# GpSimd starts with a sum over partitions before it makes the unit matrix; transposes are planned longer; the plan is searched anew

## The chip, the cores and the metric

The kernel runs on one core of a Trainium2 chip. The metric is the device time of one execution in microseconds (us); several executions are timed, and the median is the figure. One further execution is recorded by the hardware profiler, and the views shown here come from it. The engines are TensorE (PE in the profile; its weight loads are PEld), VectorE (DVE), ScalarE (ACT), GpSimd (POOL) and SyncE (SP), whose queue issues all of this kernel's DMAs.

## The reference

Causal attention in blocks of 64 over 8 batches, 8 heads, 576 positions and head width 64, then a feed-forward of two matrix products with the gate h * tanh(softplus(h)) between them, in float32:

```python
def _attn_ref(q, k, v):                       # (8, 8, 576, 64) each
    scores = scale * np.matmul(q, k.transpose(0, 1, 3, 2))
    mask = block_i >= block_j                 # blocks of 64 positions
    scores = np.where(mask, scores, -1000000000.0)
    scores = scores - np.max(scores, axis=-1, keepdims=True)
    attn = np.exp(scores)
    attn = attn / (np.sum(attn, axis=-1, keepdims=True) + 1e-09)
    return np.matmul(attn, v)

def _moe_ref(x, w_in, w_out):                 # (4608, 512), (512, 2048), (2048, 512)
    h = x @ w_in
    sp = np.where(h > 20.0, h, np.log1p(np.exp(np.minimum(h, 20.0))))
    return (h * np.tanh(sp)) @ w_out
```

The two weight matrices arrive as 64-bit words; the kernel makes float32 values of them with integer operations.

## The kernel before

**Work.** Most matrix products are done in float16 with each operand split into a high and a low half (hi and lo): three products hi*hi, hi*lo, lo*hi stand for one. Each batch has four pairs of heads and two tiles of tokens (384 and 192 columns). The first batch is computed in float32 from the loaded data directly (`attend`: scores by query L993, far blocks L1005, scores by key L1064 and L1075, subtraction of the maxima L1103, exponentials on ACT L1121, values L1136). The seven later batches go through `attend_pair`: scores S on PE (L1199, L1211), row maxima on DVE (L1240 to L1248), exponentials on ACT (L1274), the high half (L1306 or L1311; DVE, POOL or ACT) and the low half on DVE (L1323), a transpose by DMA into `PT` (L1330) and a shorter one into `PL` (L1345), and the products U with the values (L1378). Then `weigh` divides by the sums on DVE (L1441, L1442) and writes `xt`, which a DMA transposes into `x` (L1511). The feed-forward of a tile is 192 matmuls per product: `m1` (L1556), the gate on ACT (L1585), the split `Gt` on ACT or DVE (L1617, L1626, L1632), `m2` (L1661), scaling (L1693 or L1700) and a store (L1718).

**Beginning.** `make_identity` on POOL makes the unit matrix: a fill with zeros (masks.py:197) and a select that sets the diagonal (masks.py:199). ACT makes two scaled copies of it (L532), one of which, `unit_msc`, is an operand of the subtraction L1103, so PE needs it for the first pair of heads. `batch(0)` sums the squares of the first batch's v: four squares on ACT (L735), then `partition_all_reduce` on POOL adds over the partitions (L744), then DVE makes a power of two of the sum (L748, L500, L510, L750; the operation `sx`). `weight` unpacks the weights: a DMA (L574), integer operations on DVE (L583, L600), squares on ACT (L611), another sum over partitions on POOL (L619), and the halves.

**Order.** A planner sets the order of every engine before the program is built. Each operation is given an engine, a duration and the operations it waits for:

```python
unit = add("pool", 9.4, lambda: make_identity(nc, ident))
...
red = add(
    "pool", pool(4), lambda: nc.gpsimd.partition_all_reduce(TT, T, P, RED.add), sq
)
```

`pool(4)` is 0.36. `Plan.order` walks through a model of the engines and takes, on each engine, the operation with the earliest due time among those that are ready; the due times come from the table `DUE`, one number for each part of the work, and several passes backward and forward refine them. What comes out is one list in order of time, emitted operation by operation: each engine executes its own in that order and does not pass over one that waits. The DMAs' durations in the plan are pairs: the issue time on SP and the transfer's share. `TURN` is for L1330, `TURN_LATE` for L1345, `TURN_X` for L1511.

Of the kernel before, what the change touches and what calls it, by code (L numbers as in the profile page):

```python
# [18 lines left out]
RED = bass_isa.ReduceOp  # L19

P = 128
# [6 lines left out]


DUE = {  # L30
    "w": ((-46.5, 68, 288.5, 132.5), (84, 351, 228, 284.5)),
    "batch": (176, 189, 314.5, 356.5, 530.5, 736, 535.5, 733),
    "load": (
        (60.5, -52, 273, 25),
        (-74.5, 81, 78.5, -54),
        (131, 403, 308, 368.5),
        (569, 364, 410, 435),
        (393, 574, 501.5, 383.5),
        (328, 572.5, 376, 468.5),
        (511.5, 532.5, 550, 604.5),  # L40
        (521.5, 578, 675.5, 773),
        (693, 782, 838.5, 623.5),
    ),
    "tile": (
        (-92.5, -99.5, 300, -90, -20.5, -14, -31.5, -26.5,
         22, 41.5, 203.5, 303, 83.5, -150.5, 74,
         156, 263.5, 52, 27, 285, 347, 454.5),
        (332.5, 10.5, 149, 111.5, 49.5, -23.5, 20, 112,
         148, 283, 374, 296.5, 96.5, 280.5, 93,
         272.5, 290.5, 333, 290, -21.5, 267, 58),  # L50
        (122, 28.5, 413.5, 462, 420, 703.5, 334, 357.5,
         353.5, 489.5, 547, 334.5, 397.5, 225, 303,
         171, 141.5, 393, 382, 458.5, 344.5, 288),
        (665, 61, 275.5, 79.5, 406, 276, 121, 559.5,
         142, 287.5, 302.5, 256, 547.5, 15, 239.5,
         339.5, 587, 305.5, 448.5, -37, 343.5, -260.5),
        (431.5, 448, 421, 352.5, 342.5, 304.5, 403, 280.5,
         452.5, 381, 353, 234.5, 266, -52.5, 212,
         451, 597, 430.5, 440, 297, 529, 487.5),
        (90.5, 357.5, 294.5, 366, 432, 586, 536, 506,  # L60
         584, 735, 559.5, 416.5, 634, 158, 409.5,
         653, 530, 646.5, 728, 300.5, 486, 68),
        (309.5, 378, 316, 336, 489.5, 256.5, 472, 388.5,
         270, 382.5, 410.5, 511, 497.5, -59, 303,
         478, 329, 516, 402, 550.5, 630.5, 632),
        (302, 325.5, 413.5, 281.5, 390, 474, 385.5, 471.5,
         328.5, 503, 638, 491, 500, -43, 689.5,
         465, 559, 580.5, 654, 269.5, 538, 7.5),
        (493, 348.5, 293, 300, 436, 484, 596, 563.5,
         416.5, 612, 746.5, 722, 812.5, 325.5, 803,  # L70
         488, 963.5, 797.5, 736.5, 549.5, 775, 672.5),
        (514.5, 599.5, 599.5, 700, 394, 645.5, 485, 778.5,
         694.5, 844, 648.5, 631, 557, -15.5, 763,
         558.5, 600.5, 798, 580.5, -68.5, 863, -79.5),
        (858, 832, 1077.5, 882, 682, 597.5, 632, 518.5,
         727, 922, 619, 604, 917, 319, 736.5,
         958, 741.5, 957.5, 600, 661.5, 648, 614),
        (645, 469.5, 526, 1034.5, 571, 716.5, 659, 647,
         604.5, 695.5, 689, 937, 843.5, -29.5, 773.5,
         940, 1047, 695.5, 648.5, 33, 896, 35.5),  # L80
        (738.5, 602.5, 621, 678, 542, 802, 585.5, 742,
         641.5, 717.5, 619, 772.5, 950, -62.5, 740,
         894, 1029.5, 870, 758, 1016, 770.5, 1018),
        (526, 570.5, 622.5, 567.5, 569.5, 735, 846, 816,
         827, 703, 845, 749, 914, -106.5, 942,
         868, 751, 786, 699.5, -119, 1010, 10.5),
        (966.5, 995, 813, 775.5, 1067.5, 797, 1013, 1076,
         1058.5, 1155, 1276.5, 1076, 745, 30, 1197.5,
         930, 789.5, 731, 775.5, 812, 904.5, 1154),
        (796, 962.5, 907.5, 817.5, 832.5, 995, 1051, 918,  # L90
         1190.5, 1054.5, 973.5, 1032.5, 1147.5, 2, 1185,
         968.5, 1204, 994, 1112.5, 61, 1279.5, -130),
    ),
}

# [27 lines left out]
class Plan:  # L123
# [31 lines left out]
    def add(self, eng, us, emit, after=(), take=(), free=(), other=(), table=None, psum=False):  # L155

        self.ops.append(Op(eng, us, emit, after, take, free, self.due, other))
        self.ops[-1].psum = psum
        self.ops[-1].table = table
        self.ops[-1].slack = self.slack * (eng == "pe")  # L160
        return self.ops[-1]
# [186 lines left out]
def attention_moe(  # L348
# [17 lines left out]
    nc = tc.nc  # L366
# [104 lines left out]
    wmax = dv[0][:, 12:13]  # L471
# [23 lines left out]
    add = plan.add  # L495
# [31 lines left out]
    ident, *diag = (f[:, i * P : (i + 1) * P] for i in range(3))  # L527
    minus = P2[1][:, 6 * P : 7 * P]
    plan.part("w", 0, 0)
    unit = add("pool", 9.4, lambda: make_identity(nc, ident))  # L530
    units = [
        add("act", 0.2, lambda o=o, s=s: nc.scalar.mul(o, ident, s), [unit])  # L532
        for o, s in ((minus, -1.0), (unit_msc, -MSC))
# [1193 lines left out]


    SLACK = 0.7
    TURN, TURN_LATE, TURN_X = (2.15, 0.8), (1.3, 0.3), ((3.2, 1.2), (1.5, 0.5))  # L1730
    heads, tiles = {}, []

    own = [load_own(p) for p in range(NP)]
# [97 lines left out]
```

## Time and profile before

| what | value |
|---|---|
| median of 3 runs | 1016.55 us (1016.04 to 1018.67) |
| the profiled execution's own time | 1016.76 us |
| its span | 1014.9 us |
| granted TensorE clock, mean of the span | 0.991 |
| busy: PE, DVE, ACT, POOL | 985.0, 668.6, 651.1, 81.6 us |

The profiled execution lasts 1.9 us longer than its span (what lies around the first and last instruction of the program), and 0.2 us longer than the median of the runs. "Busy" leaves out the instructions that only wait, branch or issue; the releaser behind an idle time in square brackets is the instruction whose end let the engine go on, and "issue" means that the profile shows nothing that was waited for. In rows of a window come the window, its length, then busy time and number of instructions of PE, PEld, DVE, ACT and POOL, the mean granted clock of TensorE, the busy share of the 16 DMA engines and GB/s.

### The profile page before, as it was taken

The page shows a single profiled execution, that of the slowest core. Times are in us where ns is not written, and L with a number is a line of the kernel's source. Part 1 is how long each engine was busy: PE and PEld are TensorE (multiplying, and loading weights), DVE is VectorE, ACT ScalarE, POOL GpSimd, SP SyncE. Part 2 cuts the span into 40 slices and gives each one's busy share as a digit, 9 for nine tenths or more (in the row PEclk, how much of TensorE's full clock was granted, in tenths as well). Part 3 has the DMA queues.
Part 4 walks back from the last instruction along what each step waited for, and adds up shares of the span by engine and source line. Part 5 has one row for each costly group of instructions (what it writes and reads, how often), then busy time and mean ns, then how long its engine had stood idle before and what let it go on. Part 6 is the DMA issues. An engine that isn't in the chain of part 4 may idle for free.

```text
span 1014.9 us, 25319 instructions
## 1 busy us (share of the span) xinstructions
PE 985.0 (97%) x10856; PEld 732.5 (72%) x10856; DVE 668.6 (66%) x1299; ACT 651.1 (64%) x1028; POOL 81.6 (8%) x110
## 2 busy tenths in 40 slices
PE   5899899999999999999999999999999999999998
PEld 3668567686678676777777966887677776786687
DVE  2999998897687747971788877683779646120200
ACT  2578887758877856882868696585657755323221
POOL 0000221210000000110011100000011000000000
PEclk9899999999999999999999999999999999999999
DMA  8683656897487426790587746472577551240000
GB/s 275 206 252 94 176 105 135 180 167 156 86 159 159 90 52 151 161 176 24 100 170 150 172 98 134 106 140 61 113 165 149 101 105 41 37 87 1 16 17 25
DMA packets 276849, 121.58 MB, mean 120 GB/s; under 512 B 224513, under 2 KB 262913, under 8 KB 276737
## 3 DMA queue, kind: packets, MB, share of 16 engines
q1 hardware_dynamic: 276736, 119.96, 54.2%
q8 instruction: 85, 1.39, 0.6%
q14 instruction: 28, 0.22, 0.1%
HBM read 55.18 MB, written 9.44 MB: 64 GB/s over the span
## 4 chain that ended last, share of the span: by engine, by line
PE 81%; DVE 10%; issue 3%; ACT 2%; DMA 2%; SPq 1%; POOL 0%; ACTq 0%; DVEq 0%; POOLq 0%
PE acc L1661 32%; PE acc L1556 32%; PE u L1378 7%; PE ss L1199 5%; DVE P L1323 1%; DVE pv L1240 1%; DVE Gt L600 1%; PE ss L1064 1%; PE u L1136 1%; DVE Gt L1632 1%; DMA VL<-in_v_dram 1%; PE acc L664 1%; DVE wo_l L691 1%; DMA PL<-P 1%; DMA PT<-P 1%
## 5 line engine op out<-in xcount | busy, mean ns | idle before, releaser
L1556 PE MATMUL acc<-x,wi_h 128*128 128x192 f16 (+1 forms) x2048 | 395.5, 287 | 1.3 <-DMA x<-xt 1.3
L1661 PE MATMUL acc<-Gt,wo_h 128*128 128x192 f16 (+1 forms) x2048 | 385.6, 286 | 0.5 <-DVE Gt L1632 0.5
L1556 PE MATMUL acc<-x,wi_l 128*128 128x192 f16 (+1 forms) x1024 | 293.8, 287 | 0.0
L1661 PE MATMUL acc<-Gt,wo_l 128*128 128x192 f16 (+1 forms) x1024 | 292.9, 286 | 0.0
L1556 PEld LDWEIGHTS <-wi_h 128*128 128x128 f16 x2048 | 191.0, 98 | 82.2 <-issue 7.0
L1661 PEld LDWEIGHTS <-wo_h 128*128 128x128 f16 x2048 | 187.6, 98 | 52.8 <-issue 2.7
L1585 ACT ACTIVATE Et<-acc,bv 128x384 f32<-128x384 f32 x192 | 109.4, 579 | 136.2 <-PE acc L1556 135.1
L1632 DVE SCALAR_TENSOR_TENSOR Gt<-Et,bv,Gt 128x1536 f16<-128x1536 f32 (+1 forms) x64 | 92.4, 1448 | 129.4 <-ACT Gt L1617 128.8
L1274 ACT ACTIVATE pe<-ss,pv 128x192 f32<-128x192 f32 (+1 forms) x280 | 147.8, 606 | 16.9 <-DVE P L1323 8.9
L1661 PEld LDWEIGHTS <-wo_l 128*128 128x128 f16 x1024 | 100.2, 98 | 34.1 <-issue 1.2
L1556 PEld LDWEIGHTS <-wi_l 128*128 128x128 f16 x1024 | 100.4, 98 | 33.7 <-issue 0.9
L1240 DVE TENSOR_REDUCE pv<-ss 128x2 f32<-128x384 f32 (+4 forms) x140 | 105.9, 789 | 20.2 <-PE ss L1211 19.1
L1323 DVE TENSOR_TENSOR P<-pe,P 128x1024 f16<-128x1024 f32 x84 | 102.3, 1220 | 13.7 <-ACT P L1311 9.4
L1378 PEld LDWEIGHTS <-PT 128*128 128x128 f16 x2352 | 79.7, 98 | 7.8 <-issue 2.4
L1378 PE MATMUL u<-VH,PT 128*128 128x65 f16 x1568 | 82.8, 194 | 2.5 <-DVE tt L1442 2.4
L1274 ACT ACT_TABLE_LOAD x56 | 71.8, 1283 | 13.3 <-DVE pv L1248 8.7
L1378 PE MATMUL u<-VO,PT 128*128 128x64 f16 x784 | 79.4, 193 | 0.0
L1585 ACT ACT_TABLE_LOAD x58 | 74.4, 1283 | 1.0
L1617 ACT ACTIVATE Gt<-Et,bv 128x768 f16<-128x768 f32 (+1 forms) x46 | 57.1, 1241 | 12.1 <-PE acc L1661 11.1
L1700 ACT ACTIVATE ot<-acc,bv 128x384 f32<-128x384 f32 (+1 forms) x35 | 16.9, 505 | 63.9 <-PE acc L1661 56.7
L1306 POOL CAST P<-pe 128x1024 f16<-128x1024 f32 x29 | 34.6, 1193 | 198.7 <-ACT pe L1274 102.8
L1199 PEld LDWEIGHTS <-QH 64*128 64x128 f16 x896 | 27.5, 94 | 27.5 <-issue 15.5
(127 smaller groups left out, 994.5 us busy)
## 6 DMA issues: line engine op xcount, KB each, us to landing
out_dram<-ot SPq DMA_DIRECT2D x48, 192.0 KB, 2.1
wo_l<-in_w_in_dram SPq DMA_DIRECT2D x8, 1024.0 KB, 5.2
Gt<-in_w_out_dram SPq DMA_DIRECT2D x16, 512.0 KB, 4.2
kl<-in_v_dram SPq DMA_DIRECT2D x28, 288.0 KB, 3.1
ql<-in_q_dram SPq DMA_DIRECT2D x28, 288.0 KB, 3.0
kl<-in_k_dram SPq DMA_DIRECT2D x28, 288.0 KB, 3.4
VL<-in_v_dram SPq DMA_DIRECT2D x28, 192.0 KB, 2.6
VL<-in_v_dram SPq DMA_DIRECT2D x28, 96.0 KB, 2.9
```

What stands on the lines that cost most here:

```text
L1199: nc.tensor.matmul(ss[:, 512 * a + col : 512 * a + col + n], lhsT=m[q_][hs, at : at + P], rhs=m[k_][hs, key : key + n], start=first, stop= ...
L1240: nc.vector.reduce_max(out=mx[:, c], in_=ss[:, :, c0:c1], axis=mybir.AxisListType.X)
L1274: nc.scalar.activation(pe[ex[r].slot][:, cols], ss_[S0[r].slot % NSS][:, cols], AF.Exp, scale=esc, bias=mx[:, c, a : a + 1],)
L1306: return lambda: op(out=both()[0], in_=both()[2])
L1323: lambda both=both: nc.vector.tensor_sub(both()[1], both()[2], both()[0]),
L1378: nc.tensor.matmul(out, lhsT=p_, rhs=v_, start=first, stop=True, skip_group_check=True,)
L1556: nc.tensor.matmul(pt, lhsT=w[:, d, f * P : (f + 1) * P], rhs=x[:, d, :], start=k == 0 and d == 0 and z == 0, stop=d == NP - 1 and z == 2, ...
L1585: nc.scalar.activation(Et[:, (self.i * NG + g) % NE, j : j + K, 0:n], acc_[c.slot % NACC][:, 0 : K * n].rearrange("p (k n) -> p k n", k=K) ...
L1617: lambda g_hi=g_hi, ev=ev: nc.scalar.activation(g_hi, ev, AF.Copy, scale=self.s_g),
L1632: lambda g_hi=g_hi, g_lo=g_lo, ev=ev: nc.vector.scalar_tensor_tensor(out=g_lo, in0=ev, scalar=self.s_g, in1=g_hi, op0=ALU.mult, op1=ALU.su ...
L1661: nc.tensor.matmul(pt, lhsT=w[:, f, o * P : (o + 1) * P], rhs=g, start=k == 0 and f == 0 and z == 0, stop=f == NF - 1 and z == 2, skip_gro ...
L1700: evac(lambda o, i, s: nc.scalar.activation(o, i, AF.Copy, scale=s))
```

## The change

Before the unit matrix is made, POOL fills one column of `wmax` with zeros and adds it over the partitions with `partition_all_reduce`; the result is not used (`wmax` is written anew in `factors`). The unit matrix waits for that sum. The planner's figures are 9.6 for the sum and 0.9 for the unit matrix, instead of 9.4 for the unit matrix. The transposes L1330 and L1511 are planned with other durations, and the whole table `DUE` has other numbers (shown are two of its lines). Lines behind L529 move down by 3.

```diff
 DUE = {
-    "w": ((-46.5, 68, 288.5, 132.5), (84, 351, 228, 284.5)),
+    "w": ((-61.5, -2, 296, 15.5), (96.5, 301, 329, 293.5)),
...
     plan.part("w", 0, 0)
-    unit = add("pool", 9.4, lambda: make_identity(nc, ident))
+
+    nc.gpsimd.memset(wmax, 0.0)
+    warm = add("pool", 9.6, lambda: nc.gpsimd.partition_all_reduce(wmax, wmax, P, RED.add))
+    unit = add("pool", 0.9, lambda: make_identity(nc, ident), [warm])
...
     SLACK = 0.7
-    TURN, TURN_LATE, TURN_X = (2.15, 0.8), (1.3, 0.3), ((3.2, 1.2), (1.5, 0.5))
+    TURN, TURN_LATE, TURN_X = (2.7, 0.5), (1.3, 0.3), ((3.8, 0.9), (1.4, 0.5))
```

POOL's first instructions before. A row "ISA" with a line but without operands is an instruction that configures POOL: it loads the code of the instruction that follows; "ISA" with operands is the sum over partitions itself. P_99 holds the unit matrix, bv_118 the first batch's sums of squares.

```order
L420 MEMSET VH_77 128x14
L420 MEMSET VH_88 128x14
masks.py:197 MEMSET P_99 128x128
L421 MEMSET VH_77 64x4
L422 MEMSET VH_77 64x2
L421 MEMSET VH_88 64x4
L422 MEMSET VH_88 64x2
masks.py:199 ISA
masks.py:199 AFFINE_SELECT P_99<-P_99 128x128
L744 ISA
L744 ISA bv_118<-bv_118 128x4
```

The same place now (dv_123 holds `wmax`; L747 was L744):

```order
L531 MEMSET dv_123 128x1
L421 MEMSET VH_77 64x4
L422 MEMSET VH_77 64x2
L421 MEMSET VH_88 64x4
L422 MEMSET VH_88 64x2
L532 ISA
L532 ISA dv_123<-dv_123 128x1
masks.py:197 MEMSET P_99 128x128
masks.py:199 AFFINE_SELECT P_99<-P_99 128x128
L747 ISA bv_118<-bv_118 128x4
```

Two configurations have become one, which stands ahead of the new sum; the select and the first batch's sum follow it without one, and the fill of P_99 has moved behind the new sum. No later row of POOL is a configuration, before or now, up to the program's closing row.

ACT's first instructions before (P_98 receives the squares of v, PT_103 is `unit_msc`, P_99 on the left of an arrow is the negative unit matrix):

```order
L735 ACT_TABLE_LOAD
L735 ACTIVATE P_98,bv_118<-Et 128x640 x3
L532 ACTIVATE PT_103<-P_99 128x128
L735 ACTIVATE P_98,bv_118<-Et 128x640
L532 ACTIVATE P_99<-P_99 128x128
L1121 ACTIVATE pe_127<-ss_135 128x768
```

And now:

```order
L738 ACT_TABLE_LOAD
L738 ACTIVATE P_98,bv_118<-Et 128x640 x4
L535 ACTIVATE PT_103<-P_99 128x128
L535 ACTIVATE P_99<-P_99 128x128
L1124 ACTIVATE pe_127<-ss_135 128x768
```

All four squares now stand ahead of the copies of the unit matrix. On DVE the first 117 rows, on PE the first 1257 and on SP the first 58 are the same as before, but for the line numbers. The first place at which PE's order differs is the second part of the values' products U of the first pair of batch 1. Before, a chain of m1 ends and U follows (u_137 is its bank, PT_100 its transposed weights):

```order
L1556 MATMUL acc_139<-x_132,wi_h 128x192
L1556 LDWEIGHTS wi_l
L1556 MATMUL acc_139<-x_132,wi_l 128x192
L1378 LDWEIGHTS PT_100
L1378 MATMUL u_137<-VH_77,PT_100 128x65
L1378 LDWEIGHTS PT_100
L1378 MATMUL u_137<-VO_78,PT_100 128x64
```

Now the first scores of the third pair (ss_135 their bank) come between; U follows behind them (L1381):

```order
L1559 MATMUL acc_139<-x_132,wi_h 128x192
L1559 LDWEIGHTS wi_l
L1559 MATMUL acc_139<-x_132,wi_l 128x192
L1202 LDWEIGHTS QH_71
L1202 MATMUL ss_135<-KH_73,QH_71 128x128
L1202 LDWEIGHTS QH_71
L1202 MATMUL ss_135<-KH_73,QH_71 128x128
```

These 22 matmuls of scores stood behind U before. From here on the orders of all engines go apart; the instructions of PE are the same in number and shape. Of the other work some casts change engine: high halves (L1306 on DVE and POOL, L1311 on ACT) go from 37, 29 and 18 on DVE, POOL and ACT to 32, 25 and 27, and splits `Gt` (L1626 on DVE, L1617 on ACT) from 18 and 46 to 11 and 53.

More of the change, by code (lines that the diff above doesn't have):

```diff
@@ L30 @@
 DUE = {
-    "w": ((-46.5, 68, 288.5, 132.5), (84, 351, 228, 284.5)),
-    "batch": (176, 189, 314.5, 356.5, 530.5, 736, 535.5, 733),
+    "w": ((-61.5, -2, 296, 15.5), (96.5, 301, 329, 293.5)),
+    "batch": (134.5, 54, 455.5, 305.5, 387.5, 808, 492, 726.5),
     "load": (
[L34 to L42, printed above, removed]
+        (83.5, -32, 600.5, 570),
+        (36, 483.5, 361.5, -83.5),
+        (276, 346.5, 611, 481.5),
+        (565, 598, 494.5, 672.5),
+        (648.5, 658, 422.5, 604),
+        (343, 499, 528.5, 422.5),
+        (661.5, 543, 581, 672),
+        (519.5, 843, 510.5, 637.5),
+        (757.5, 795, 760, 591.5),
@@ L43 @@
     ),
     "tile": (
[L45 to L89, printed above, removed]
@@ L90 @@
-        (796, 962.5, 907.5, 817.5, 832.5, 995, 1051, 918,
-         1190.5, 1054.5, 973.5, 1032.5, 1147.5, 2, 1185,
-         968.5, 1204, 994, 1112.5, 61, 1279.5, -130),
+        (-51, -125.5, -73.5, -80.5, -51, -47.5, -51, -26.5,
+         319, 223.5, 300.5, 333, 81.5, -56.5, 375,
+         314.5, 398.5, 467, 26.5, 342, 505.5, 522),
+        (19.5, 249.5, 135.5, 297.5, 196.5, -21.5, 316, 400.5,
+         604.5, 539.5, 679, 458.5, 343, 123.5, 283.5,
+         267, 250.5, 470, 358, -216, 356.5, -75),
@@ new lines @@
+        (320, 282.5, 449, 284, 681, 964, 780, 427,
+         447, 435.5, 624, 399.5, 375.5, 484, 386.5,
+         320.5, 409.5, 543, 531.5, 375, 412.5, 340),
+        (483, 31, 275.5, 339.5, 292.5, 104, 293, 625,
+         84.5, 303.5, 373.5, 407, 379.5, -72.5, 127,
+         404, 404.5, 421, 565.5, -125.5, 356, -251.5),
+        (448.5, 373.5, 590, 365.5, 434.5, 336.5, 446.5, 284,
+         357.5, 489.5, 428, 310, 292.5, -42, 410,
+         513.5, 777.5, 590, 613, 604, 709.5, 639.5),
+        (372.5, 551, 292.5, 381.5, 476.5, 835, 556, 396.5,
+         724, 871, 821, 711.5, 554.5, 463.5, 309,
+         893, 680.5, 615, 529, 515, 441.5, 30),
@@ new lines @@
+        (373, 388, 435, 502.5, 260, 301.5, 656.5, 579,
+         297.5, 503, 548, 528, 666, 511, 332,
+         627, 392, 426, 519.5, 752, 584.5, 605.5),
+        (368, 598.5, 373, 367.5, 583, 554.5, 411, 406,
+         237.5, 328.5, 607.5, 573, 674.5, -33.5, 787,
+         729, 772.5, 818.5, 923.5, 63.5, 469.5, -66),
+        (389, 453, 304.5, 478, 715, 634, 371.5, 693.5,
+         348, 796.5, 774, 602.5, 855.5, 503, 530,
+         776, 701.5, 819, 590, 813, 895, 812.5),
+        (634.5, 956, 494.5, 795, 1165, 830.5, 1058, 709,
+         710, 839.5, 692.5, 741.5, 725, 247.5, 944.5,
+         560, 629.5, 1001, 527.5, -160, 671, -106),
@@ new lines @@
+        (802.5, 973, 1047, 434.5, 658.5, 854, 632, 826,
+         762, 798, 686, 941, 746.5, 271.5, 1046.5,
+         667, 865, 1006, 611, 643, 1168.5, 645),
+        (832, 643.5, 951.5, 1059, 547.5, 819, 763.5, 866,
+         699, 730.5, 1083.5, 1171.5, 1010.5, -12, 856,
+         594.5, 1149, 860.5, 1071.5, -34, 790, -55.5),
+        (944.5, 712, 595.5, 736, 871.5, 785.5, 960.5, 607,
+         692, 788, 586.5, 1165.5, 977.5, 12.5, 753,
+         572.5, 900.5, 937.5, 839.5, 768.5, 725.5, 796.5),
@@ new lines @@
+        (1028.5, 640, 726, 558, 695.5, 664, 1160.5, 1140.5,
+         1094.5, 925, 768.5, 853, 1007, -98, 1008,
+         1061.5, 723, 870, 774.5, -89, 1203.5, 261.5),
+        (950.5, 896.5, 636, 989.5, 884, 689.5, 926, 1069,
+         955.5, 1107, 1099.5, 940.5, 677.5, -156, 1045.5,
+         851.5, 705.5, 754.5, 1035.5, 839, 1052, 1161),
+        (794, 1058.5, 678.5, 694.5, 811.5, 1135, 639, 810.5,
+         937.5, 1100.5, 1138.5, 870.5, 1130.5, -151.5, 1101,
+         876, 1045, 1214.5, 1347.5, 355.5, 1319.5, 461),
```

## The prediction

> **What bounds the kernel now.** I read the page first, then the busy time by stages, with the stages cut where the idle times of PE end; then the chain of waits; then the timeline of each engine at the place that it pointed to.
>
> The page's span and first line of busy times:
>
> ```profile
> span 1014.9 us, 25319 instructions
> PE 985.0 (97%) x10856; PEld 732.5 (72%) x10856; DVE 668.6 (66%) x1299; ACT 651.1 (64%) x1028; POOL 81.6 (8%) x110
> ```
>
> The stages:
>
> ```profile
> 18.20:27.10 8.90, 0.01 (x1) 0.00 (x0) 4.89 (x12) 0.36 (x1) 0.44 (x1) 0.63 0.47 151
> 27.10:40.00 12.90, 12.19 (x108) 9.84 (x110) 12.31 (x31) 7.17 (x10) 0.50 (x1) 0.86 0.81 277
> 40.00:144.00 104.00, 97.65 (x856) 68.39 (x852) 100.99 (x201) 83.66 (x127) 12.36 (x16) 0.97 0.60 165
> 144.00:242.00 98.00, 92.65 (x1248) 70.90 (x1248) 85.16 (x169) 72.00 (x123) 19.63 (x17) 1.00 0.76 152
> 242.00:1011.00 769.00, 768.96 (x8565) 573.25 (x8562) 461.03 (x867) 480.65 (x755) 46.95 (x61) 1.00 0.50 102
> ```
>
> The chain of waits in order of time (start, length, what):
>
> ```profile
> 14.51 6.97 issue
> 21.48 0.45 POOL bv L744
> ...
> 242.00 15.60 PE acc L1556 x96
> ```
>
> The reader should see three stages. From 242 us to 1011 us PE has work for 768.96 of 769.00 us, and this is real work: the chain's row of 96 matmuls of 384 columns in 15.60 us is 0.1625 us each, without gaps. Nothing there can be made shorter by an order; an order can only spoil it. From 27 to 144 us DVE is the fuller engine (100.99 of 104.00 us), and whatever sets DVE free earlier moves this stage as a whole. And from 18.2 to 27.1 us PE stands still, and the chain of waits shows why: 6.97 us of "issue" ahead of POOL's sum L744. The page alone (PE 97%) hides this, since 8.9 us is under 1% of the span.
>
> The timeline at that place (start, length, instruction), of POOL:
>
> ```profile
> 1.31 0.24 POOL masks.py:197 MEMSET P<- 128x128 f32 x1
> ...
> 2.09 0.10 POOL L422 MEMSET VH<- 64x2 f16 x1
> 10.85 0.28 POOL masks.py:199 TENSOR_SCALAR_AFFINE_SELECT P<-P 128x128 f32<-128x128 f32 x1 [8.66 <-issue]
> 21.48 0.44 POOL L744 PARTITION_ALL_REDUCE bv<-bv  x1 [10.34 <-issue]
> ```
>
> Of ACT, DVE and PE:
>
> ```profile
> 11.17 0.31 ACT L532 ACTIVATE PT<-P 128x128 f16<-128x128 f32 x1
> 11.39 0.72 ACT L735 ACTIVATE P<-Et 128x640 f32<-128x640 f32 x1
> ...
> 12.01 0.19 ACT L735 ACTIVATION_READ_ACCUMULATOR P<-Et 128x1 f32 x1
> 12.13 1.46 PE L1103 MATMUL ss<-PT,PT 128*128 128x128 f16 x12
> ...
> 17.51 0.70 PE L993 MATMUL acc<-Et 64*128 64x256 f32 x2
> ...
> 21.95 0.16 DVE L748 TENSOR_REDUCE bv<-bv 128x1 f32<-128x4 f32 x1 [11.68 <-POOL bv L744]
> ...
> 22.73 0.68 DVE L583 TENSOR_SCALAR wo_h<-wo_l 128x1024 int32<-128x1024 int32 x1
> ...
> 25.85 1.41 DVE L1023 TENSOR_REDUCE PT<-acc 128x1 f32<-128x384 f32 x4
> ...
> 27.12 0.79 PE L993 MATMUL acc<-Et 64*128 64x256 f32 x1 [8.91 <-DVE PT L1023]
> ...
> 29.80 0.75 DVE L1023 TENSOR_REDUCE PT<-acc 128x1 f32<-128x256 f32 x2
> ...
> 30.58 0.17 DVE L1036 TENSOR_SCALAR PT<-PT 128x6 f16<-128x6 f32 x1
> ...
> 30.99 0.84 PE L1103 MATMUL ss<-PT,PT 128*128 128x128 f16 x12
> ...
> 39.53 0.69 DVE L583 TENSOR_SCALAR wo_h<-wo_l 128x1024 int32<-128x1024 int32 x1
> ```
>
> POOL waits twice for nothing that the profile shows, each time behind a configuration: 8.66 us ahead of the select and 10.34 us ahead of the sum. The squares that the sum adds were there at 12.20 us (12.01 + 0.19). DVE stands at L748, 11.68 us; queued behind it are the unpacking L583 and the maxima L1023, for which PE waits 8.91 us.
>
> **The change part by part.** *The code loads.* One of the two goes. The remaining one is that of the sum over partitions, so I take that routine's own row, 10.34 us; the other end is the 8.66 us that a load took at this very place. It begins when the fills end, at 2.09 + 0.10 = 2.19 us. The load ends at 12.53, the new sum takes 0.44 (12.97), the fill that has moved behind it 0.24 (13.21), the select 0.28 (13.49), the first batch's sum 0.44 (13.93). With 0.1 us for each of three handovers (an estimate; L748 began 0.03 us behind the end of L744) DVE can begin L748 at about 14.2 us rather than 21.95: 7.7 us earlier. At the short end the load is over at 10.85 and the select at about 12.0, the squares are ready too (12.20 less the 0.31 of the copy L532 that has moved behind them), and L748 begins at 12.5: 9.4 us earlier.
>
> What is late next: the weights for L583, which stood 0.78 us behind the beginning of L748. Their loads up to 24 us, and the DMA engines in two windows (columns as above):
>
> ```profile
> L574 SPq DMA_DIRECT2D wo_l<-in_w_in_dram x2: 440/458/477, 7.6 to 8.1; - x2
> ...
> DMA to landing us min/median/max: 5.9/8.8/10.6
> ```
>
> ```profile
> 12.00:22.00 10.00, 6.21 (x54) 5.12 (x51) 0.04 (x1) 1.91 (x5) 0.44 (x1) 0.92 1.04 376
> 22.00:26.00 4.00, 0.00 (x0) 0.00 (x0) 3.75 (x9) 0.36 (x1) 0.00 (x0) 0.50 0.01 2
> ```
>
> The first part, issued at 7.6, landed 5.9 us later at the earliest, at 13.5. That is ahead of 14.2 + 0.8, and caps the short end at 22.73 - 13.5 = 9.2 us. Until 22 us the transfers fill the DMA engines (1.04); then nothing moves (0.01), because the next load waits for DVE. Now that load is issued about 8 us earlier, behind the burst: 1 MB at 376 GB/s takes 2.8 us, so it is there by about 25, and DVE uses it at 39.53 - 7.7 = 31.8. Cost nothing; its cover is DVE's own queue.
>
> *The unit matrix gets later.* It was ready at 11.13 (10.85 + 0.28), now at 13.5 to 13.6. Its copy L532 (0.31) then releases the subtraction L1103 on PE at about 14.0 instead of 12.13, 1.9 us later. PE's block up to 18.21 (17.51 + 0.70) then ends at 20.1, while DVE would release PE at 27.12 - 7.7 = 19.4. So PE comes 0.7 us late to that point; but DVE needs its products only at 29.80 - 7.7 = 22.1, 2.0 us behind PE's new start, and before, at half the clock, 2.7 us (27.12 to 29.80) were enough for DVE not to wait. DVE stays the later one, and L1103 of the second pair, which starts behind L1036, moves from 30.99 to 23.3. Cost: nothing, as long as DVE is the later.
>
> *The new fill and sum* cost 0.1 and 0.44 us of POOL, counted above. No other queue carries them.
>
> *The clock.* The idle 8.9 us had the granted clock at 0.63, and the 12.9 us behind it at 0.86, a loss of 0.14 * 12.9 = 1.8 us of PE's work. I give no gain for it, since DVE, not PE, sets the pace there. The Trainium skill, "TensorE: Matmul & The Clock Gate", Part 1, says that an idle window of about 3.4 us halves the clock until PE has been busy as long again; the trace agrees (0.50 from 22 to 26 us). By that page alone the sum would be up to 1.8 us better.
>
> *The transposes and the new order.* Until 144 us the order is the old one; the time of this stage moves as a block. In the next stage PE stood 98.00 - 92.65 = 5.35 us.
>
> Its waits by releaser (total us, times, longest), then two rows of PE's timeline and the transposes' row (issue times in ns: min/median/max):
>
> ```profile
> PE u L1378 <- DVE tt L1442: 2.4, 3, 1.1
> PE ss L1199 <- ACT pe L1274: 1.7, 2, 1.5
> PE acc L1556 <- DMA x<-xt: 1.1, 1, 1.1
> PE acc L1661 <- DVE Gt L1632: 0.5, 2, 0.3
> ```
>
> ```profile
> 136.66 0.19 PE L1378 MATMUL u<-VH,PT 128*128 128x65 f16 x1
> ...
> 144.72 0.20 PE L1378 MATMUL u<-VH,PT 128*128 128x65 f16 x1 [1.10 <-DVE tt L1442]
> ```
>
> ```profile
> L1330 SPq DMA_TRANSPOSE PT<-P x84: 1332/2824/4597, 113.7 to 886.7; - x84
> ```
>
> The wait of 1.10 us at 144.72 is where the order first differs: 22 matmuls of scores now fill it. I take 0.8 us of it as gained. The plan's 2.7 us for issuing L1330 is nearer to the median of 2.82 than 2.15 was, which argues for fewer surprises, but what the new order makes of the other waits no row shows: bounds are minus 5.35 us (all gone) and plus 5.35 us (twice as much). I take zero, since the same DVE work (85.16 of 98 us) stands in nearly the same order. Behind 242 us there is nothing to gain; the upper bound of a loss is that stage's kind of wait once more, some 2.4 us.
>
> **The sum.** 7.7 + 0.8 = 8.5 us off the profiled execution's own 1016.76 (span 1014.9 and 1.9 around it) gives 1008.3; the median lies 0.2 under that execution: 1008.0 us.
>
> **The rivals.**
> 1. *The gain is partly lost later* (11%). DVE's lead shrinks in the stage to 242 us, or the new order opens waits of PE in the dense stage, because more casts went to ACT: 9 high halves and 7 splits.
>
> ```profile
> L1311 ACT CAST P<-pe 128x1024 f16<-128x1024 f32 x18 | 18.7, 1040 | 13.4 <-DMA PT<-P 5.6 <-DMA PL<-P 5.5 <-issue 1.9
> L1274 ACT ACT_TABLE_LOAD x56 | 71.8, 1283 | 13.3 <-DVE pv L1248 8.7 <-DVE dv L1441 3.7
> ```
>
> With 3 to 5 us lost this gives 1011 to 1013.5. Against it: ACT was busy 480.65 of 769.00 us there.
> 2. *More is gained* (11%): the short load (9.2) and most of the 5.35 us gone: 1016.55 - 13 = 1003.5, or the clock's 1.8 us on top of 9.2: 1005.5.
> 3. *The load is not saved* (5%). If the select needs its own code although no configuration stands ahead of it, 8.66 us come back before the unit matrix: 12.97 + 0.24 + 8.66 + 0.28 = 22.2, the first sum ends at 22.7 against 21.92, and PE's block of 6.1 us ends at 28.8 against the release at 27.12: 0.8 to 1.7 us longer, about 1018. The trace has no sum and select side by side, so it doesn't exclude this; the order, with one configuration less, speaks against it. The Trainium skill, "GPSIMD Engine Reference", section 2.1, says that the first call to a freshly loaded kernel pays a load of about 6 us that no instruction shows. Here the two cost 8.66 and 10.34 us. By that page a first call of the select would pay again: 2.19 + 6 + 0.44 + 0.24 + 6 + 0.28 = 15.2, L748 at 15.8, 6.1 us earlier than before, and a time of about 1010; without the second payment the weights' 9.2 us would be the gain.
> 4. *Slower* (3%). PE starves behind ACT in the dense stage: its three banks cover 3 * 12 * 0.1625 = 5.85 us without an evacuation. A table load (1.28) and two casts (1.04 each) more in one block of ACT, 3.4 us, can pass that. To outweigh 8.5 us and be seen, 11.6 us are needed: four such places of 3 us. Time: 1020 to 1022. Against it: no wait of PE for ACT behind 242 us is in the trace.
>
> **How the numbers follow.** The forecast itself, 1005 to 1011 (startup 7.7 to 9.2, the second stage within 2 us), has 70%. The range, 1004.5 to 1012.0, takes in half of rivals 1 and 2, 81% in all. A measurement of this kernel tells about 0.3%, 3.05 us, from no change: faster is below 1013.5. Faster holds the forecast and rivals 1 and 2: 92%; within 0.3% is most of rival 3: 5%; slower is rival 4 and the rest of 3: 3%.
>
> **What would show it.** Right: POOL has one idle of 8.7 to 10.4 us and L747 (was L744) starts at 12 to 14 us; DVE's wait at L751 is 2.4 to 4 us instead of 11.68; PE's 8.91 us idle is under 2 us and its granted clock stays at 1.00 from 18 to 40 us; the first part of U (L1381) of batch 1 begins near 129 rather than 136.66 us; PE is full from about 234 us to the end. Wrong: a second idle of POOL ahead of the select (rival 3), waits of PE for ACT or for transposes after 234 us (1, 4), or a stage up to 234 us with clearly more than 5 us of idle PE.

## The result and the profile after

The changed kernel takes 1006.6 us (median of 7 runs, 1004.75 to 1012.87), the kernel before 1016.93 us beside it (7 runs, 1016.04 to 1018.67): a ratio of 0.9904, 95% interval 0.988 to 0.9928, or 7.3 to 12.2 us less. The profiled execution took 1007.62 us, 9.14 less than that of before, and its span shrank by 9.4 us. The first lines of its page:

```profile
span 1005.5 us, 25329 instructions
...
PE 986.4 (98%) x10856; PEld 734.6 (73%) x10856; DVE 662.2 (66%) x1288; ACT 664.4 (66%) x1042; POOL 83.5 (8%) x111
```

The timeline of POOL at its beginning (start, length, instruction, idle before it and what ended that):

```profile
2.00 0.10 POOL L422 MEMSET VH<- 64x2 f16 x1
2.23 0.39 POOL L532 PARTITION_ALL_REDUCE dv<-dv  x1
2.48 0.28 POOL masks.py:197 MEMSET P<- 128x128 f32 x1
2.84 0.29 POOL masks.py:199 TENSOR_SCALAR_AFFINE_SELECT P<-P 128x128 f32<-128x128 f32 x1
11.84 0.44 POOL L747 PARTITION_ALL_REDUCE bv<-bv  x1 [8.71 <-ACT P L738]
```

No wait for "issue" is left: not one of the two loads went, but both. The new sum begins 0.13 us behind the last fill although a configuration stands ahead of it, and the unit matrix is ready at 3.13 us instead of 11.13. POOL then waits 8.71 us for something real, ACT's squares.

DVE's timeline behind that sum:

```profile
12.31 0.16 DVE L751 TENSOR_REDUCE bv<-bv 128x1 f32<-128x4 f32 x1 [2.00 <-POOL bv L747]
...
14.79 0.69 DVE L586 TENSOR_SCALAR wo_h<-wo_l 128x1024 int32<-128x1024 int32 x1 [1.62 <-DMA wo_l<-in_w_in_dram]
...
17.92 1.41 DVE L1026 TENSOR_REDUCE PT<-acc 128x1 f32<-128x384 f32 x4
...
26.75 1.42 DVE L1026 TENSOR_REDUCE PT<-acc 128x1 f32<-128x384 f32 x4 [1.56 <-PE acc L1008]
```

PE's timeline at the same place, and its first products U of batch 1:

```profile
13.55 2.08 PE L996 MATMUL acc<-Et 64*128 64x384 f32 x8
...
15.67 5.38 PE L1139 MATMUL u<-Et,pe 128*128 128x65 f32 x24
...
25.52 1.14 PE L996 MATMUL acc<-Et 64*128 64x384 f32 x8
...
26.64 2.89 PE L1139 MATMUL u<-Et,pe 128*128 128x65 f32 x24
...
130.36 0.19 PE L1381 MATMUL u<-VH,PT 128*128 128x65 f16 x1
```

The reader can follow how the gain shrinks. On DVE, L751 is 9.64 us earlier than L748 was (12.31 against 21.95), and the unpacking L586 only 7.94 us (14.79 against 22.73), since the first part of the weights isn't there: 1.62 us of wait. But in this execution that wait does not set the pace. PE works from 12.2 to 26.6 us without a gap, DVE's next maxima at 26.75 wait 1.56 us for it, and the chain of waits (start, length, what), shown below a row of that window (columns as in the stages further down; the clock, third from the end, reads 1.00), runs through PE:

```profile
12.20:26.60 14.40, 14.40 (x97) 11.80 (x96) 10.55 (x22) 3.63 (x6) 0.07 (x1) 1.00 1.06 377
```

```profile
12.22 1.40 PE ss L1106 x12
13.62 2.01 PE acc L996 x8
...
15.74 5.31 PE u L1139 x24
...
26.66 0.10 PE acc L1008 x4
26.76 1.41 DVE PT L1026 x4
```

PE is slow there: the same eight matmuls take 2.08 us at 13.55 and 1.14 at 25.52, the same 24 take 5.38 and then 2.89. It runs at half its rate until about 24 us. Before, those 24 took 2.89 us already at 14.69. So U at 130.36 is only 6.30 us earlier (136.66 before), held back by PE; had the weights come sooner, PE would have been no faster.

The stages, cut 8 to 10 us earlier than those of before (window, length, then PE, PEld, DVE, ACT, POOL, granted clock, DMA share, GB/s), and PE's waits by releaser from 136 to 234 us:

```profile
32.00:136.00 104.00, 97.59 (x852) 68.27 (x853) 100.94 (x204) 83.67 (x125) 13.04 (x16) 0.97 0.59 166
136.00:234.00 98.00, 94.40 (x1266) 73.12 (x1264) 86.84 (x171) 73.60 (x125) 12.66 (x15) 1.00 0.77 156
234.00:1001.50 767.50, 767.34 (x8566) 572.02 (x8563) 454.44 (x854) 494.10 (x770) 54.76 (x63) 1.00 0.50 103
```

```profile
PE acc L1664 <- DVE ot L1696: 1.2, 1, 1.2
PE acc L1664 <- DVE Gt L1635: 1.1, 1, 1.1
PE ss L1202 <- DVE tt L1445: 1.0, 1, 1.0
PE acc L1559 <- DVE ot L1696: 0.3, 1, 0.3
```

PE stands for 3.60 us in the second stage (98.00 - 94.40) instead of 5.35, and for other reasons: the waits of U for `tt` and of the scores for ACT are gone, and waits of m2 and of the scores have taken their place. From 234 us PE is full, 767.34 of 767.50 us. From the first U to the end it took 1014.9 - 136.66 = 878.2 us before and 1005.5 - 130.36 = 875.1 now. So in this execution the 9.4 us are 6.3 from the beginning and 3.1 behind U. Of these 3.1, some 2.0 are idle time of PE (878.24 - 868.59 = 9.65 us before, 875.10 - 867.41 = 7.69 now); the rest is busy time, less by 1.2 us for the same work, and no row shows why.

### The profile page after: what moved, and what is told of

The parts are those of the page before. It is cut to its first block, busy times and chain, and to the rows that moved or that the text cites. A ratio compares the mean times of both kernels' runs of the same rounds, so it can differ in the third digit from the quotient of the medians.

```text
span 1005.5 us, 25329 instructions
## 1 busy us (share of the span) xinstructions
PE 986.4 (98%) x10856; PEld 734.6 (73%) x10856; DVE 662.2 (66%) x1288; ACT 664.4 (66%) x1042; POOL 83.5 (8%) x111
## 4 chain that ended last, share of the span: by engine, by line
PE 87%; DVE 8%; ACT 2%; issue 2%; DMA 1%; SPq 1%; DVEq 0%; ACTq 0%
PE acc L1664 36%; PE acc L1559 33%; PE u L1381 7%; PE ss L1202 5%; PE u L1139 2%; DVE Gt L603 1%; PE ss L1067 1%; DVE pv L1243 1%; DVE P L1326 1%; PE acc L996 1%; DMA PT<-P 1%; PE acc L667 1%; DVE wo_l L694 1%; PE ss L996 1%; PE ss L1106 0%
## 5 line engine op out<-in xcount | busy, mean ns | idle before, releaser
L1381 PEld LDWEIGHTS <-PT 128*128 128x128 f16 x2352 | 79.7, 98 | 4.7 <-issue 0.6
L1381 PE MATMUL u<-VH,PT 128*128 128x65 f16 x1568 | 82.8, 194 | 0.0
L1381 PE MATMUL u<-VO,PT 128*128 128x64 f16 x784 | 79.4, 193 | 0.0
L1620 ACT ACTIVATE Gt<-Et,bv 128x768 f16<-128x768 f32 (+1 forms) x53 | 64.8, 1224 | 15.7 <-PE acc L1664 14.6
L1202 PEld LDWEIGHTS <-QH 64*128 64x128 f16 x896 | 27.5, 95 | 26.6 <-issue 14.0
L1309 DVE CAST P<-pe 128x1024 f16<-128x1024 f32 x32 | 22.8, 714 | 34.0 <-DMA PT<-P 23.6
```

What stands on the lines that cost most here:

```text
L1202: nc.tensor.matmul(ss[:, 512 * a + col : 512 * a + col + n], lhsT=m[q_][hs, at : at + P], rhs=m[k_][hs, key : key + n], start=first, stop= ...
L1309: return lambda: op(out=both()[0], in_=both()[2])
L1381: nc.tensor.matmul(out, lhsT=p_, rhs=v_, start=first, stop=True, skip_group_check=True,)
L1620: lambda g_hi=g_hi, ev=ev: nc.scalar.activation(g_hi, ev, AF.Copy, scale=self.s_g),
```

## Why both loads are gone

A configuration of POOL asks for a set of code, which can serve more than one kind of instruction. Whether it loads that set each time is the question here.

The kernel before goes through two sets of code in every execution: it begins with that of the select, then configures that of the sum. The changed kernel needs only the sum's set, and the select ran in it. Theory R: POOL keeps its code from one execution to the next. Before, each execution found the sum's set where the select's was wanted, and paid twice; now it finds what it needs and pays nothing. Theory N: a configuration ahead of a sum costs nothing by itself and only the one ahead of the select was dear. One instruction at the very end tells them apart, since it leaves another set behind:

```diff
     with tc.manual_schedule():
         for o in ops:
             o.emit()
+        nc.gpsimd.tensor_tensor(
+            out=VL[:, 6, 0:1], in0=VL[:, 6, 0:1], in1=VL[:, 6, 1:2], op=ALU.add
+        )
```

*In the changed kernel* (e3_other_code_last):

> The changed kernel with one more instruction on POOL at its very end: an addition of two columns of a tile that is no longer used, which needs another set of code than the sum over partitions. Its result is used by nothing. Theory R (POOL keeps its code from one execution to the next; the change gains because its only set is still there): the next execution must load again at its start, so an idle time of 8 to 12 us stands ahead of the new sum at L532 (it was at 2.23 us, now at 10 to 14.5), the first batch's sum L747 begins at 12 to 16 instead of 11.84, and the time is 0 to 3 us above the changed kernel's 1006.6. The other theory, N (a configuration that stands ahead of a sum over partitions and ahead of nothing else costs no load): the new sum stays at 2.2 us and the time within 0.5 us of 1006.6.

POOL at the beginning of the next execution:

```profile
9.62 0.40 POOL L532 PARTITION_ALL_REDUCE dv<-dv  x1 [7.53 <-issue]
...
12.79 0.44 POOL L747 PARTITION_ALL_REDUCE bv<-bv  x1 [2.26 <-ACT P L738]
```

The load is back, 7.53 us ahead of the new sum (8 to 12 us were expected). But the time is 1005.16 us (6 runs, 1004.16 to 1011.83; ratio 0.9877, 0.9847 to 0.9908), no more than the changed kernel's, where theory R had been given 0 to 3 us more. One load costs nothing measurable here: it ends at 9.62, and the squares, for which the first batch's sum still waits 2.26 us, come later.

*In the kernel before* (e4_before_other_code_last):

> The kernel before with the same added instruction at its very end (its result is used by nothing). The two configurations at the start stay. Theory R: the select finds its set still loaded from the end of the previous execution and runs at 2.5 to 3.5 us instead of 10.85; only the sum's load of 8.7 to 12.4 us is left, from about 3 us, so L744 begins at 12 to 16 instead of 21.48 and the time falls from 1016.9 to 1008 to 1012. Theory N, or any in which each configuration loads: both waits stay, L744 at about 21.5, and the time within 1 us of 1016.9.

```profile
2.48 0.29 POOL masks.py:199 TENSOR_SCALAR_AFFINE_SELECT P<-P 128x128 f32<-128x128 f32 x1 [0.29 <-POOL VH L422]
12.99 0.45 POOL L744 PARTITION_ALL_REDUCE bv<-bv  x1 [10.22 <-ACT P L735]
```

With both configurations still in their places, with the old plan and without any new sum at the start, the select runs at 2.48 instead of 10.85 and the sum at 12.99 instead of 21.48; a load of the sum's own set, if there is one, is hidden in a wait of 10.22 us for the squares, so this run doesn't show its length. The time is 1008.27 us (6 runs, 1007.0 to 1011.96; ratio 0.9904, 0.9874 to 0.9933). Theory R gave both profiles, though the load of e3 was shorter than it said, and theory N neither. In these two comparisons the kernel before had a median of 1019.64 us, in the others 1016.93 to 1017.05; against 1016.9 the gain of e4 is 8.6 us. So what gives the gain of the beginning is that no more than one load stands ahead of the first batch's sum; that the second is gone too brings nothing that e3 could measure. The runs repeat one kernel; what another kernel in between would leave on POOL was not measured.

## The two parts of the change, each alone

Theory A: the whole gain is the beginning. Theory B: the new plan carries a third of it. (C and D are on the clock, below.)

*The sum alone* (e1_sum_only): the kernel before, with its old table and its old durations of the transposes, and only this:

```diff
-    unit = add("pool", 9.4, lambda: make_identity(nc, ident))
+    nc.gpsimd.memset(wmax, 0.0)
+    warm = add("pool", 9.6, lambda: nc.gpsimd.partition_all_reduce(wmax, wmax, P, RED.add))
+    unit = add("pool", 0.9, lambda: make_identity(nc, ident), [warm])
```

> The kernel before with the new fill and sum ahead of the unit matrix alone; old due times, old durations of the transposes. PE, DVE and SP have the order of before word for word, so what is gained is the code load's share. If the whole gain of the change is the start (theory A: POOL's two waits go, the rest of the new plan is worth nothing): 1006 to 1008, and PE idle between 136 and 234 us stays near 5.4 us. If the new plan carries about a third (theory B: 6.3 us from the start, some 3 us from the stage behind): 1009.5 to 1011. In both the first sum on POOL starts at about 2.2 us without a wait if the code is still there from the execution before, and DVE's L751 at about 12.3 us.

1008.14 us (6 runs, 1006.55 to 1012.33; before 1016.95), ratio 0.992, 0.9896 to 0.9943: 8.1 us less, between 5.8 and 10.6. The median lies between the two ranges, close to A's. Its profiled execution, with PE at full rate from 13.3 us on, reaches U at 126.50, 10.2 us earlier than before, and takes 1005.0 - 126.50 = 878.5 us from there to the end, as before (878.2): the sum acts on the beginning alone. Its longest waits of PE for the old order are still there:

```profile
PE u L1381 <- DVE tt L1445: 2.8, 3, 1.4
```

*The plan alone* (e2_plan_only): the changed kernel with that edit undone.

> The changed kernel without the new fill and sum: the unit matrix first again (planned 9.4), the new due times and the new durations of the transposes. PE, DVE and SP have the order of the changed kernel word for word. Theory A: 1016 to 1017.5, no difference from before. Theory B: 1013 to 1015, with the two idle times of POOL (about 8.7 and 10.3 us) back and PE idle behind 144 us some 3 us less than before.

1014.1 us (12 runs, 1013.19 to 1019.32), ratio 0.9978, 0.9961 to 0.9994: 2.2 us less, between 0.6 and 4.0. Its POOL shows that the loads' lengths are not fixed; both are longer here than in the kernel before:

```profile
12.43 0.28 POOL masks.py:199 TENSOR_SCALAR_AFFINE_SELECT P<-P 128x128 f32<-128x128 f32 x1 [10.24 <-issue]
25.06 0.44 POOL L744 PARTITION_ALL_REDUCE bv<-bv  x1 [12.36 <-issue]
```

From U, which it reaches at 139.25, to the end it takes 1015.8 - 139.25 = 876.6 us, 1.6 less than before. Its PE stands 98.00 - 93.89 = 4.11 us between 146 and 244 us, 1.2 less than the 5.35 of before; some 3 us less had been expected.

8.1 and 2.2 us add up to the 9.8 of the changed kernel's ratio, within their intervals. The plan's part is a good fifth of the whole (2.2 of 9.8). Its interval just leaves out theory A's zero and takes in theory B's third (3.3 us).

## The clock and the first weights

Two things could have shortened the gain in the profiled execution: PE's half rate up to 24 us, and the wait for the weights. Theory C: the first costs about 1.5 us; theory D: it costs nothing.

*A warm PE* (e5_warm_pe): 58 matmuls on data that need no load are issued first, into the bank of U, which is written anew before it is read.

```diff
     with tc.manual_schedule():
+        for _ in range(58):
+            nc.tensor.matmul(
+                u_[0][:, 0:P], lhsT=far_q, rhs=far_own, start=True, stop=True,
+                skip_group_check=True,
+            )
         for o in ops:
             o.emit()
```

> The changed kernel with 58 matmuls of 128 columns ahead of everything on PE (their result is overwritten), about 6.2 us at half clock, from about 1.8 to 8 us. In the changed kernel's trace the clock first shows as full at 24.3 us and the values of the first pair (24 matmuls, L1139) took 5.38 us, in the trace of before 13.6 us and 2.89 us. If the late clock is what cost 1.5 us of the start (theory C): the clock is full by 9 us, those 24 matmuls take 2.9 us, DVE's wait of 1.56 us for PE at 26.8 us is gone, and the time is 1004 to 1006, with a smaller spread between runs. If the clock doesn't matter because DVE and the weights set the pace (theory D): no change or, since the first scores start some 3.4 us later, up to 3 us longer, 1007 to 1010.

1005.41 us (5 runs, 1003.86 to 1005.7), ratio 0.9881, 0.9861 to 0.9901. That looked like C, and as if the scatter of the changed kernel's times were gone. So I tried it with the first half-MB of w_in ahead of the second pair's q and k (e6_warm_and_weight), that reordering alone (e7_weight_first), and the changed kernel again (e8_changed_again):

```diff
     ops = plan.order()
+    at = [i for i, o in enumerate(ops) if o.eng == "sp"]
+    ops.insert(at[10], ops.pop(at[12]))
```

> The warmed kernel (58 matmuls on PE at the start, whose result is written anew before it is read), and the first half-MB of w_in is issued ahead of the second pair's q and k instead of behind them. Expected if the wait for that part (1.91 us of DVE at L586 with the warm PE) is on the path that sets the end: the wait goes, the first S at L1202 moves from 93.2 to 91.3, and the time from 1005.4 to 1003.5 to 1004. Rival: the second pair's q and k land 1.4 us later, PE's first L996 of that pair waits for them and DVE for PE, and the time stays within 0.5 us of 1005.4.

> The changed kernel with that reordering of the loads alone and no warmed PE. If the scatter of the changed kernel (1004.75 to 1012.87) comes from PE's clock at the start, it stays here (lowest 1003, highest above 1009) while the one with the warm PE lies within 2.5 us; if it comes from the time at which the first weights land, this kernel scatters less and the clock has nothing to do with it.

> The changed kernel once more, unaltered, beside the two others. Its time: 1006.6, scattered from 1004.7 to 1013. In each of its runs the mean clock and the span are there: if the clock at the start makes the scatter, a run with a mean clock of 0.998 lies near 1005 and one with 0.993 or less above 1008.

DVE in e6:

```profile
13.55 0.15 DVE L753 TENSOR_SCALAR bv<-bv 128x1 f32<-128x1 f32 x1
13.62 0.68 DVE L586 TENSOR_SCALAR wo_h<-wo_l 128x1024 int32<-128x1024 int32 x1
```

The wait for the weights is gone, as meant, and the time isn't shorter: 1005.53 us (6 runs, 1003.72 to 1010.51; ratio 0.9885, 0.986 to 0.991). e7 has 1009.41 us (6 runs, 1004.01 to 1014.7; 0.9918, 0.9886 to 0.995), e8 1006.57 (6 runs, 1003.2 to 1013.12; 0.9899, 0.9867 to 0.9932). So the weights' landing alone doesn't make the scatter; nor do the six runs of e6 lie within 2.5 us, as expected if PE's clock at the start made it. The runs of e8 go with their mean clock as expected: 1003.2, 1004.16, 1006.61 and 1006.53 us at 0.996 to 0.997, 1011.72 and 1013.12 at 0.990 and 0.988. Others do not: 1011.83 us at 0.997 (e3), 1009.11 at 0.997 (e7), 1006.41 at 0.993 (e10). The mean clock is a poor witness here, because the column can read 1.00 while PE runs at half rate (12.20 to 26.60 us above). Last, the warmed kernel and the changed one side by side, both unaltered:

> The warmed kernel (58 matmuls on PE at the start) once more, unaltered, beside the changed kernel. If the warm PE is what narrows the scatter, its runs lie between 1003.5 and 1006.5, with at most one outside; if the narrow scatter of its five first runs was chance, it scatters to 1010 and more.

> The changed kernel, unaltered, beside the warmed one. If the warm PE narrows the scatter, two or three of its six runs lie above 1008 and its median is 1 to 2 us above that of the warmed kernel; if not, the medians are within 0.5 us.

The warmed kernel has 1008.53 us (6 runs, 1003.37 to 1011.91; ratio 0.9894, 0.9864 to 0.9924), the changed one 1006.9 (6 runs, 1006.33 to 1009.81; 0.9892, 0.9869 to 0.9914). Both expectations of a warm PE that narrows the scatter were missed: the warmed kernel reached 1011.91, and its median lay above the changed one's. The narrow scatter of e5 was chance, by these six runs. Over 11 runs the warmed kernel's median is 1005.6, over 19 runs the changed kernel's 1006.6, and each covers some 8 to 10 us. That no version beats the changed kernel by what can be measured is the outcome here.

But the profiled execution of e9 was one of the long ones, 1011.91 us, and shows where they lose time. Windows of it:

```profile
18.50:35.70 17.20, 16.27 (x88) 13.33 (x90) 12.43 (x33) 6.28 (x9) 0.40 (x1) 0.50 0.91 308
...
132.60:1009.80 877.20, 867.53 (x9889) 649.72 (x9887) 547.81 (x1037) 574.42 (x903) 68.71 (x79) 1.00 0.53 109
```

PE was warm by then; a wait of 1.84 us for DVE's maxima ended at 19.43, and from about 18.6 to 35.7 us the granted clock was 0.50 although PE was busy for 16.27 of 17.20 us. U, which e9 reaches at 132.6, comes at 126.77 in the profiled execution of e8, whose PE runs at the full rate from the second pair on:

```profile
13.50 1.14 PE L996 MATMUL acc<-Et 64*128 64x384 f32 x8
...
14.62 2.89 PE L1139 MATMUL u<-Et,pe 128*128 128x65 f32 x24
...
126.77 0.19 PE L1381 MATMUL u<-VH,PT 128*128 128x65 f16 x1
```

Against 136.66 before that is 9.9 us of gain at the beginning instead of 6.3, and a span of 1001.2 us. Of the 8.6 us between the spans of e8 and e9 (1001.2, 1009.8) 5.8 had arisen before U. L586 began at 15.03 in e9 and at 13.60 in e8, 1.4 us later; how much of that reached U behind the slow PE is not shown. A second place is in e3 (its profiled execution took 1011.83 us), in its windows:

```profile
185.00:192.00 7.00, 5.01 (x81) 4.49 (x81) 4.98 (x22) 5.41 (x10) 0.99 (x1) 0.76 1.03 178
```

There a wait of 2.04 us of m2 for `ot` (L1696) ended at 186.99, and the clock fell for half of the window: an estimate of 3.4 us (0.24 * 7.00 / 0.5). All profiled executions side by side show that the scatter arises both ahead of U and behind it (U to the end is the span less U):

| profiled execution | plan | U, us | U to the end, us |
|---|---|---|---|
| before | old | 136.66 | 878.2 |
| e1, the sum alone | old | 126.50 | 878.5 |
| e4 | old | 127.63 | 878.5 |
| changed kernel | new | 130.36 | 875.1 |
| e8, changed again | new | 126.77 | 874.4 |
| e10, changed again | new | 129.34 | 878.5 |
| e3 | new | 131.08 | 878.5 |
| e2, the plan alone | new | 139.25 | 876.6 |
| e5, warm PE | new | 128.18 | 875.4 |
| e9, warm again | new | 132.58 | 877.2 |
| e6 | new | 127.07 | 877.0 |
| e7 | new | 126.27 | 876.7 |

With the old plan the stretch behind U is the same to 0.3 us; with the new plan it varies by 4.1 us, from nothing gained to 3.8 us gained. The wait for `ot` near 185 us is part of that: no profiled execution of the old plan has it, and with the new plan it lasts from nothing (e8) to 2.31 us (e7). Ahead of U a good part of the difference is half-rate time of PE (the changed kernel, e3, e9). The warm-up matmuls don't remove it, because the idle time that precedes it in e9 comes after them. What decides whether such a wait lowers the clock, and for how long, stays open: the profiled execution of e5 had a wait of 1.57 us for the same maxima and kept its clock; that of e10 had one of 1.68 us, and the clock was 0.87 from 17.00 to 19.00 and 0.67 from 19.00 to 23.40 us, by estimate 3.4 us of half rate instead of the 17 of e9.

## The prediction, step by step

*One of two code loads goes, the other costs 8.66 to 10.34 us.* This step failed in its mechanism: no load was paid, because the price of a configuration depends on what the execution before left behind (e3, e4). POOL's one idle time of 8.71 us lies inside the 8.7 to 10.4 that I had named as a sign, by luck: it ended with ACT's squares, not with a load. I had read the two "issue" waits as the price of two instructions. By the rule of the Trainium skill, "GPSIMD Engine Reference", section 2.1, that I quoted, a first call pays about 6 us; no call of the changed kernel paid, and where one did (e3) it was 7.53.

*L751 at 14.2 us, 7.7 us earlier.* It was 12.31, near the short end of 12.5, and DVE waited 2.00 us for it, not 2.4 to 4. What sets it isn't a load but the squares, done at about 11.8; I had them ready at 11.89 (12.20 - 0.31). In e3, where a load was paid, the sum came less than a microsecond later (12.79), and there too behind the squares. So the wrong mechanism cost the forecast little: the 10.34 us given to the remaining load are what made 14.2 too late.

*The weights cap the gain at 9.2 us.* The step is right for DVE, mis-sized in number: L586 waited for them and came 7.94 us earlier, since they landed at about 14.7 (issued at 7.4, 7.3 us to landing) instead of 13.5. That the wait's removal in e6 brought nothing measurable, and that U came 9.9 us earlier in e8 and 10.2 in e1, more than the cap, says that it isn't the last bound.

*The unit matrix gets later and PE stays ahead of DVE; the clock brings nothing.* The matrix came 8 us earlier. That DVE stays the later one failed in the profiled execution: at half rate PE was late by 1.56 us and the gain fell to 6.3 us. My condition, that this costs nothing "as long as DVE is the later", held in e1 and e8 but not here. The full clock that I expected "from 18 to 40 us" began at about 24, although the column reads 1.00 before.

*U near 129 us*: 130.36, and 126.77 in e8. *PE's 8.91 us idle under 2 us*: 0.3 us in all. *PE full from about 234 us*: right.

*The second stage gives 0.8 us.* It gave 3.1 us behind U in the profiled execution and 2.2 us (0.6 to 4.0) by e2, but nothing in the profiled execution of e10 (878.5). In the former the wait for `tt` that I priced went, and so did the two others of its row (2.4 us in all); what came in their place was shorter. One number for this term was too simple: it changes from execution to execution.

So 7.7 + 0.8 became 6.3 + 3.1. That the total of 8.5 us is close to the 9.14 of the profiled execution is in part luck: a load that was not paid, PE's slow clock and a larger gain behind U cancelled, and no term came out as stated. Of the rivals, a second load ahead of the select (1018) is refuted by the select at 2.84 us; a loss in the dense stage and a slower kernel through ACT by 0.16 us of idle PE behind 234 us. The rival of a greater gain is what the shortest executions show (1003.2 us, e8), through an early full clock and the shortest stretch behind U (874.4 us).

## What to carry to other kernels

What POOL loads ahead of its first instructions depended here on what the previous execution left loaded: look at the last instruction of the program as well as the first, and aim at one set of code throughout, or at an end whose set is the one that the beginning wants. Behind a removed wait stands the next one, here squares, weights and the rate of PE; price each before you credit the wait's whole length. A single profiled execution of a kernel that can run at two clock rates is one draw: cut several at the same landmark, as with U above, before you credit a small edit.

## What the runs showed of the hardware

- POOL's code outlived the execution: the same configuration ahead of a sum cost 7.53 us with another set left behind, and nothing measurable with its own. The loads that were paid lasted 7.53 (e3), 8.66 and 10.34 (before), 10.24 and 12.36 us (e2).
- The select ran behind the sum over partitions without a load (2.84 us, no wait). The addition at the end of e3 and e4 leaves another set behind: the next execution's sum waited 7.53 us (e3), while the next select waited for no load (2.48 us, e4).
- Half rate can last long under load: 17 us in e9 with PE 95% busy (16.27 of 17.20). The Trainium skill, "TensorE: Matmul & The Clock Gate", Part 1, states that the full clock is back after some 3.4 us of busy PE; the trace of e9 disagrees, and so does that of the changed kernel, whose PE works without a gap from 12.2 us and is at half rate up to about 24; those of e3 and e10 agree (3.4 us each, by the estimates above).
- The column of the granted clock can hide a slow start: in the changed kernel it reads 1.00 from 12.20 to 26.60 us while PE ran at half rate up to about 24. The only sign of it is the length of equal matmuls (24 of them 5.38 us at 15.67 and 2.89 at 26.64), which is the surer reading.
